# Cross-attention followed by a gated feed-forward on one core: scores, sums and first softmax product of batch 3 one loop step later

## The chip, the core and the metric

The kernel runs on one core of a Trainium2 chip. The core has five engines with a queue of instructions each: TensorE (PE in the profile; its weight loads are shown as PEld), VectorE (DVE), ScalarE (ACT), GpSimd (POOL) and SyncE (SP), which here only issues DMAs. An engine takes its instructions strictly in the order in which they were written; between engines there are semaphores only. The metric is the time of one execution on the device, in microseconds; the time before is 223.09 us, the median of three runs.

## The reference

Everything is for 8 batches and 8 heads, with 512 rows of x and 32 rows of state of width 64 in each head. Both directions of attention are computed, their results stand one under the other, and all 4352 rows of width 512 go through a gated feed-forward.

```
scores  = softmax(x @ state^T / 8)        # 512 x 32 in each head
xread   = scores @ state
sread   = softmax(state @ x^T / 8) @ x    # 32 x 64 in each head
y       = concat([xread, sread])          # 8*(512+32) rows of 512
out     = (sigmoid(y @ w_gate) * (y @ w_val)) @ w_out   # 512 -> 1536 -> 512
```

## The kernel before

The row maximum is not subtracted. The exponentials E of the scores are computed once and serve both directions: divided by their sums over the state rows they are the weights of xread, and used as the stationary operand against x they give sread. xread itself is never formed. For each batch the kernel multiplies the state with both weight matrices (SW, lines 255 to 303) and then multiplies the transposed softmax (aT) with SW, which gives gate and value directly. The sigmoid is a tanh on ScalarE (`gv_th`, L327) and one VectorE operation that adds 1 and multiplies with the value (`gv_glu`, L332); the factor 0.5 follows at the output.

The order of all instructions is written out by hand. After a long start-up for batches 0 to 2, the main loop runs b from 2 to 8 (b=8 stands for the sread rows of all batches) and, in each pass, twelve steps f of 128 hidden columns. A step has two parts on TensorE: the gate and value set of batch b (`gv_mm`, four matmuls at L317) and a third of an output tile of batch b-1 (`out_mm`, four matmuls at L348). Between them the pass prepares the next batch, nb = b+1. For nb the steps before the change do this:

- f=0 and f=6: `sw_wide`, the SW products of half the hidden columns (L259, L266), into PSUM banks that VectorE and ScalarE empty over the following steps (`sw_cp`, L303).
- f=1 and f=2: `S_mm` (eight matmuls at L147), the scores of two of the four column chunks of the batch each, into the one PSUM bank of pool `p_at` (AT), and `S_exp` (L167), their exponential on ScalarE. Score set i reads chunks 2i and 2i+1 of xT, the transposed x of nb.
- f=2 and f=3: `n_sum` (L181, L183), sums and reciprocals on VectorE. f=3: `at_Eb` (L173), four casts of E to bf16 on GpSimd.
- f=4 and f=6: `n_mul` (L200), the two softmax products on VectorE. f=5 and f=6: `aT_dma` (L221), two transposing DMAs each, from SP.
- f=6: `rd_mm` (L235 for batch 3 on), the sread product, which reads all four casts; `rd_fin` (L246, L248) writes xr, and `rd_dma` (L251) transposes it into XS. In the pass b=2 three more `rd_dma` follow at f=8.
- x is loaded two batches ahead by SP (`load_x`, L78), cast by GpSimd (`cast_x`, L116) and transposed by four DMAs from SP, one for each chunk (`at_xT_dma`, L140). For nb=3 the load of batch 5 is at f=3 and cast and transposes of batch 4 at f=6; for all other batches these are at f=0 and f=1. Batch 3's own x transposes are issued ahead of the loop.

In each step the gate and value set takes the two PSUM banks of pool `p_gv` in turn: the gate bank comes free when L327 has read it, the value bank when L332 has. SP also issues the stores of the output (L356). Its DMAs wait in one queue in the order of the program.

Of the kernel before, what the change touches and what calls it, by code (L numbers as in the profile page):

```python
# [16 lines left out]
def kernel(  # L17
# [50 lines left out]
    AT, OU, GV, SWP = (p_at, "at"), (p_out, "outp"), (p_gv, "gv"), (p_sw, "swp")  # L68
# [33 lines left out]
    def gate(landed):  # L102

        nc.gpsimd.tensor_copy(pre[:, 1:2], landed)  # L104
# [37 lines left out]
    def S_mm(b, i, place, jjs=(0, 1)):  # L142
        if b > 1:
            ps = held["S", b, i] = place[0].tile((128, 2, 2, 4, Ns), FP, name="Sp", tag=place[1])
            for c in range(2):
                for j in range(4):
                    nc.tensor.matmul(ps[:, c, :, j], xTs[b][:, j, 2 * i + c], sTz[:, b, j], start=True, stop=True)  # L147
            return
        if jjs[0] == 0:
            held["S", b, i] = place[0].tile((128, 4, 2, 2, Ns), FP, name="Sp", tag=place[1])  # L150
        ps = held["S", b, i]
        for jj in jjs:
            j = 2 * i + jj
            for c in range(4):
                e, c2 = c // 2, c % 2 * 2
                nc.tensor.matmul(ps[:, c2:c2 + 2, e, jj], xTs[b][:, j, c], sTd[:, b, 2 * j + e], start=True, stop=True)

    def half(b, i, t):

        if b > 1:  # L160
            return t[b][:, 2 * i:2 * i + 2].rearrange("p c e (j n) -> p (c e j) n", n=Ns)
        return t[b].rearrange("p c e (j n) -> p (c e) j n", n=Ns)[:, :, 2 * i:2 * i + 2]

    def S_exp(b, i):
        if b not in E1s:
            E1s[b] = ap_.tile((128, 4, 2, 128), FP, name="E1")
        nc.scalar.activation(half(b, i, E1s), held["S", b, i].rearrange("p c e j n -> p (c e j) n" if b > 1 else "p c e j n -> p (c e) j n"),  # L167
                             AF.Exp, scale=scale)
# [6 lines left out]
    def grp(b, t):  # L175

        return t if b > 1 else t.rearrange("p (g j) -> p g j", j=2)

    def n_sum(b, i):
        rs = ap_.tile((128, 16), FP, name="rs")  # L180
        nc.vector.tensor_reduce(grp(b, rs), half(b, i, E1s), AX.X, ALU.add)  # L181
        ri = held["ri", b, i] = ap_.tile((128, 16), FP, name="ri")
        nc.vector.reciprocal(ri, rs)  # L183
# [12 lines left out]
    def n_mul(b, i, eng):  # L196
        if b not in abs_:
            abs_[b] = ap_.tile((128, 4, 2, 128), BF, name="ab")
        ri, e1 = grp(b, held["ri", b, i]), half(b, i, E1s)
        (nc.gpsimd if eng is pool else nc.vector).tensor_tensor(half(b, i, abs_), e1,  # L200
                          ri.unsqueeze(len(ri.shape)).to_broadcast(e1.shape), ALU.mult)
# [7 lines left out]
    def aT_tile(b):  # L209
        if b not in aTs:  # L210
            aTs[b] = ap_.tile((128, 4, 2, 128), BF, name="aT")
        return aTs[b]
# [6 lines left out]
    def aT_dma(b, i):  # L219
        for c in range(2 * i, 2 * i + 2):  # L220
            nc.sync.dma_start_transpose(aT_tile(b)[:, c], abs_[b][:, c].rearrange("p e k -> p (e k)"))  # L221
# [4 lines left out]
    def rd_mm(b, place):  # L226

        ps = place[0].tile((128, 512), FP, name="rdp", tag=place[1])
        rd = held["rd", b] = ps[:, :2 * D + 2].rearrange("p (e d) -> p e d", e=2)
        for e in range(2):  # L230
            for c in range(4):
                for j in range(4):
                    h, o, Eb = 2 * j + e, rd[j * Ns:(j + 1) * Ns, e], Ebs[b][:, c, e, j * Ns:(j + 1) * Ns]
                    if b > 2:
                        nc.tensor.matmul(o, Eb, xs[:, c, h, :D + 1], start=(c == 0), stop=(c == 3))  # L235
                    else:
                        xh = xhs[b][:, h, c] if b in xhs else xbs[b][:, c, h]
                        nc.tensor.matmul(o[:, :D], Eb, xh, start=(c == 0), stop=(c == 3))  # L238
        for e in range(2 if b < 3 else 0):
            for c in range(4):  # L240
                nc.tensor.matmul(rd[:, e, D:], Ebs[b][:, c, e], ones, start=(c == 0), stop=(c == 3))

    def rd_fin(b):
        rd = held["rd", b]
        r2 = ap_.tile((128, 2, 1), FP, name="rr")
        nc.vector.reciprocal(r2, rd[:, :, D:])  # L246
        xr = held["xr", b] = ap_.tile((128, 2, D), BF, name="xr", bufs=4)
        nc.vector.tensor_tensor(xr, rd[:, :, :D], r2.to_broadcast((128, 2, D)), ALU.mult)  # L248

    def rd_dma(b):  # L250
        nc.sync.dma_start_transpose(XS[:, b].rearrange("p j n -> p (j n)"), held["xr", b].rearrange("p e d -> p (e d)"))  # L251
# [33 lines left out]
    def sw_wide(b, v, other=AT):  # L285

        if b not in SWs:
            SWs[b] = fp.tile((128, 2, 2, dff), BF, name="SW", bufs=2)
        lo = 768 * v
        for k, places in enumerate(((OU, other), (SWP, SWP), (SWP, SWP))):  # L290
            pss = [p[0].tile((128, 512), FP, name="swp", tag=p[1]) for p in places]
            if k < 2:
                sw_mm(pss, b, k, lo, 512, 0)
            else:
                sw_pair(pss, b, lo + 512, 256)
            for e in range(2):
                if k < 2:
                    sw_left[b, v, k, e] = (SWs[b][:, e, k, lo:lo + 512], pss[e])
                else:
                    sw_left[b, v, k, e] = (SWs[b][:, e, :, lo + 512:lo + 768], pss[e].rearrange("p (w n) -> p w n", w=2))  # L300

    def sw_cp(b, lo, w, e, cp):
        cp(*sw_left.pop((b, lo, w, e)))  # L303
# [20 lines left out]
    def gv_th(b, f):  # L324

        th = held["th", b, f] = fp.tile((128, 512), FP, name="th")[:, :n_of(b)]
        nc.scalar.activation(th, held["gv", b, f][0], AF.Tanh, scale=0.5)  # L327

    def gv_glu(b, f):
        if b not in glus:  # L330
            glus[b] = fp.tile((128, NF, n_of(b)), BF, name="glu", bufs=2, padded_shape=(128, NF, 512))
        nc.vector.scalar_tensor_tensor(glus[b][:, f], held["th", b, f], 1.0, held["gv", b, f][1], ALU.add, ALU.mult)  # L332
# [349 lines left out]
    for b in range(2, B + 1):  # L682
        nb = b + 1 if b + 1 < B else None
        for f in range(NF):

            v, q = divmod(f, 6)
            ahead = nb is not None and q == 0
            if ahead:
                if v:
                    rd_mm(nb, AT)  # L690
                sw_wide(nb, v, GV if v else AT)
                if v:
                    n_mul(nb, 1, nc.vector)
                    rd_fin(nb)
                sw_cp(nb, v, 0, v, act)
                sw_cp(nb, v, 0, 1 - v, act)
            for first in (ahead, not ahead):
                if first:
                    gv_mm(b, f, SWP if b == B and f % 2 else GV)
                    gv_th(b, f)  # L700
                    gv_glu(b, f)
                elif b < B or f < 9:
                    out_mm(b - 1, f)
            if nb is not None:
                if f in (0, 8):
                    sw_cp(nb, v, 1, 0, vec)
                if q in (1, 3, 4):
                    k = max(q + 1, 3)
                    sw_cp(nb, v, k // 2, k % 2, act)
                if f in (1, 2):  # L710
                    S_mm(nb, f - 1, AT)
                    S_exp(nb, f - 1)
                if f in (2, 3):
                    n_sum(nb, f - 2)
                elif f == 4:
                    n_mul(nb, 0, nc.vector)
                if f == 3:
                    at_Eb(nb)
                if f == (3 if nb == 3 else 0) and nb + 2 < B:
                    load_x(nb + 2, nc.sync)  # L720
                if f in (5, 6):
                    aT_dma(nb, f - 5)
                if f == 6:
                    rd_dma(nb)
                if b == 2 and f == 8:
                    for q in range(3):
                        rd_dma(q)
                if f == 0:
                    gate(held["th", b, 0][:, 0:1])
                    cast_xs(nb, 0, 4)  # L730
                    cast_xs(nb, 4, 4)
                if f == (6 if nb == 3 else 1) and nb + 1 < B:
                    cast_x(nb + 1, pool, 0, 4)
                    cast_x(nb + 1, pool, 4, 4)
                    at_xT_dma(nb + 1)
# [33 lines left out]
```

## Time and profile before

| | us |
|---|---|
| runs before, median (lowest, highest) | 223.09 (222.89, 224.12) |
| profiled execution | 223.65 |
| its span, first to last instruction | 221.9 |
| TensorE busy | 214.9 |
| ScalarE busy | 129.0 |
| VectorE busy | 118.3 |
| GpSimd busy | 53.8 |

The profile is of one execution. Times in it are counted from the start of the span; an engine's line in the order of time gives the start, the length, the engine, the line of the kernel, the operation, the tile written and the tiles read, how many such instructions are merged, and in brackets how long the engine sat idle before and what ended that. Consecutive instructions overlap a little, since their pipelines do; the advance of an engine is read from start to start. SPq is SP's queue of DMA issues; a DMA's landing is the time from its issue to the arrival of its data.

### The profile page before, as it was taken

The page shows a single profiled execution, that of the slowest core. Times are in us where ns is not written, and L with a number is a line of the kernel's source. Part 1 is how long each engine was busy: PE and PEld are TensorE (multiplying, and loading weights), DVE is VectorE, ACT ScalarE, POOL GpSimd, SP SyncE. Part 2 cuts the span into 40 slices and gives each one's busy share as a digit, 9 for nine tenths or more (in the row PEclk, how much of TensorE's full clock was granted, in tenths as well). Part 3 has the DMA queues.
Part 4 walks back from the last instruction along what each step waited for, and adds up shares of the span by engine and source line. Part 5 has one row for each costly group of instructions (what it writes and reads, how often), then busy time and mean ns, then how long its engine had stood idle before and what let it go on. Part 6 is the DMA issues. An engine that isn't in the chain of part 4 may idle for free.

```text
span 221.9 us, 4663 instructions
## 1 busy us (share of the span) xinstructions
PE 214.9 (97%) x1801; PEld 103.8 (47%) x1801; DVE 118.3 (53%) x209; ACT 129.0 (58%) x241; POOL 53.8 (24%) x90
## 2 busy tenths in 40 slices
PE   7799999999989999999999999999999999999994
PEld 2454444443444444444444454445444444466744
DVE  1889897476365546744484358353754344322301
ACT  5678877367655657656774857566756444433311
POOL 8787110470514036001800090005100000000001
PEclk9999999999999999999999999999999999999999
DMA  6999999852799555955462205420132111111113
GB/s 194 193 203 195 268 228 161 159 186 60 77 286 307 53 124 140 207 140 178 141 177 46 95 3 132 103 74 30 47 84 67 47 49 62 62 68 47 52 29 113
DMA packets 41910, 27.11 MB, mean 122 GB/s; under 512 B 24000, under 2 KB 38080, under 8 KB 41888
## 3 DMA queue, kind: packets, MB, share of 16 engines
q1 hardware_dynamic: 32544, 18.95, 36.3%
q0 software_dynamic: 9056, 7.67, 19.8%
q8 instruction: 14, 0.23, 0.4%
q10 hardware_dynamic: 288, 0.20, 0.4%
q14 instruction: 8, 0.07, 0.1%
HBM read 18.35 MB, written 8.91 MB: 123 GB/s over the span
## 4 chain that ended last, share of the span: by engine, by line
PE 89%; DMA 7%; SPq 2%; issue 0%; ACT 0%; POOL 0%; DVE 0%
PE gvp L317 37%; PE outp L348 37%; PE gvp L320 5%; PE swp L259 4%; DMA wgv<-in_moe_w_gate_dram 3%; DMA xT<-xb 2%; DMA xf<-in_x_dram 2%; SPq L140 2%; PE swp L266 2%; PE outp L370 1%; PE Sp L147 1%; PE rdp L235 1%; SPq L83 0%; PE stp L410 0%; PE rdp L238 0%
## 5 line engine op out<-in xcount | busy, mean ns | idle before, releaser
L332 DVE SCALAR_TENSOR_TENSOR glu<-th,gvp 128x512 bf16<-128x512 f32 (+1 forms) x108 | 70.5, 657 | 85.1 <-ACT th L327 68.9
L348 PE MATMUL outp<-wo,glu 128*128 128x512 bf16 x396 | 98.2, 379 | 0.0
L317 PE MATMUL gvp<-aT,SW 128*128 128x512 bf16 x384 | 96.6, 379 | 0.0
L327 ACT ACTIVATE th<-gvp 128x512 f32<-128x512 f32 (+1 forms) x108 | 61.7, 574 | 59.9 <-PE gvp L317 47.6
L317 PEld LDWEIGHTS <-SW 128*128 128x128 bf16 x384 | 36.2, 98 | 47.7 <-issue 5.6
L348 PEld LDWEIGHTS <-glu 128*128 128x128 bf16 x396 | 37.8, 98 | 42.2 <-issue 0.4
L303 ACT CAST SW<-swp 128x512 bf16<-128x512 f32 x70 | 39.2, 584 | 6.3 <-PE swp L259 4.7
L352 ACT ACTIVATE res<-outp 128x512 f32<-128x512 f32 x33 | 19.7, 597 | 15.0 <-PE outp L348 15.0
L104 POOL COPY pre<-th 128x1 f32<-128x1 f32 x5 | 0.9, 188 | 70.8 <-ACT th L327 70.8
L303 DVE CAST SW<-swp 128x512 bf16<-128x512 f32 x26 | 17.3, 684 | 1.1 <-PE swp L266 0.8
L361 POOL DMA_DIRECT2D out_dram<-res x2 | 1.1, 550 | 60.4 <-ACT res L352 60.4
L173 POOL CAST Eb<-E 128x256 bf16<-128x256 f32 x32 | 11.8, 402 | 12.0 <-ACT E L167 12.0
L116 POOL CAST xb<-xf 128x1024 bf16<-128x1024 f32 x10 | 10.6, 1087 | 11.2 <-DMA xf<-in_x_dram 7.3
L320 PE MATMUL gvp<-XS,wgv 128*128 128x256 bf16 x96 | 11.9, 273 | 0.0
L167 ACT ACTIVATE E<-Sp 128x512 f32<-128x512 f32 x16 | 9.5, 603 | 3.1 <-PE Sp L147 1.9
L320 PEld LDWEIGHTS <-wgv 128*128 128x128 bf16 x96 | 9.4, 98 | 3.0
L224 POOL CAST xs<-xf 128x1024 bf16<-128x1024 f32 x10 | 10.2, 1046 | 0.0
L181 DVE TENSOR_REDUCE rs<-E 128x16 f32<-128x512 f32 x14 | 9.4, 673 | 1.2 <-ACT E L167 1.2
L200 DVE TENSOR_TENSOR ab<-E,ri 128x512 bf16<-128x512 f32 x13 | 9.1, 709 | 0.0
L259 PE MATMUL swp<-wgv,sTc 64*32 64x512 bf16 x192 | 7.6, 381 | 0.0
L384 PE MATMUL warm<-wm 128*128 128x512 bf16 x17 | 6.0, 472 | 1.0 <-DVE wm L431 1.0
L147 PEld LDWEIGHTS <-xT 128*128 128x128 bf16 x96 | 4.4, 98 | 3.5 <-DMA xT<-xb 0.9
(71 smaller groups left out, 92.3 us busy)
## 6 DMA issues: line engine op xcount, KB each, us to landing
out_dram<-res SPq DMA_DIRECT2D x24, 256.0 KB, 3.1
xf<-in_x_dram SPq DMA_DIRECT2D x4, 1024.0 KB, 6.6
xf<-in_x_dram POOLq DMA_DIRECT2D x2, 1024.0 KB, 8.9
out_dram<-res SPq DMA_DIRECT2D x15, 128.0 KB, 1.9
wo<-in_moe_w_out_dram POOLq DMA_DIRECT2D x3, 512.0 KB, 13.7
xf<-in_x_dram SPq DMA_DIRECT2D x4, 256.0 KB, 4.0
wgv<-in_moe_w_gate_dram POOLq DMA_DIRECT2D x2, 512.0 KB, 8.5
wgv<-in_moe_w_val_dram POOLq DMA_DIRECT2D x2, 512.0 KB, 10.0
```

The source lines that it names most:

```text
L116: cp(xbs[b].rearrange("p c h d -> p h c d")[:, lo:lo + n], (xhs if b in xhs else xfs)[b][:, lo:lo + n])
L167: nc.scalar.activation(half(b, i, E1s), held["S", b, i].rearrange("p c e j n -> p (c e j) n" if b > 1 else "p c e j n -> p (c e) j n"), AF ...
L173: nc.gpsimd.tensor_copy(Ebs[b][:, c], E1s[b][:, c])
L224: pool(xs.rearrange("p c h d -> p h c d")[:, lo:lo + n, :, :D], xfs[b][:, lo:lo + n])
L259: nc.tensor.matmul(pss[e][j * Ns:(j + 1) * Ns, o:o + n], sTc[rows, b, j] if b > 1 else sTd[rows, b, 2 * j + e, e], (wg, wv)[w][rows, j, lo ...
L303: cp(*sw_left.pop((b, lo, w, e)))
L317: nc.tensor.matmul(ps, SWs[b][:, g, w, fs], aTs[b][:, :, g], start=(g == 0), stop=(g == 1))
L320: nc.tensor.matmul(ps, (wg, wv)[w][:, j, fs], XS[:, :, j], start=(j == 0), stop=(j == 3))
L327: nc.scalar.activation(th, held["gv", b, f][0], AF.Tanh, scale=0.5)
L332: nc.vector.scalar_tensor_tensor(glus[b][:, f], held["th", b, f], 1.0, held["gv", b, f][1], ALU.add, ALU.mult)
L348: nc.tensor.matmul(ops[b, c], glus[b][:, f, c * 128:(c + 1) * 128], wo[:, f], start=(f == 0), stop=(f == NF - 1))
L352: nc.scalar.activation(res, ops[b, c], AF.Copy, scale=0.5)
```

## The change

For nb=3 only, the steps of the chain scores, exponential, sums, first softmax product and casts move by one: g = f-1 takes the place of f. The score sets go to f=2 and f=3, the sums to f=3 and f=4, the casts to f=4, the first product to f=5 and the first pair of aT transposes to f=6, where the second pair already stands. The second product, the sread product and its transpose, all SW work, loads, casts of x and their transposes keep their steps. For all other batches g = f, and the order is as before. Within a step the order of the calls stays.

```diff
-                if f in (1, 2):
-                    S_mm(nb, f - 1, AT)
-                    S_exp(nb, f - 1)
-                if f in (2, 3):
-                    n_sum(nb, f - 2)
-                elif f == 4:
+                g = f - 1 if nb == 3 else f
+                if g in (1, 2):
+                    S_mm(nb, g - 1, AT)
+                    S_exp(nb, g - 1)
+                if g in (2, 3):
+                    n_sum(nb, g - 2)
+                elif g == 4:
                     n_mul(nb, 0, nc.vector)
-                if f == 3:
+                if g == 3:
                     at_Eb(nb)
                 if f == (3 if nb == 3 else 0) and nb + 2 < B:
                     load_x(nb + 2, nc.sync)
-                if f in (5, 6):
-                    aT_dma(nb, f - 5)
+                if g == 5:
+                    aT_dma(nb, 0)
                 if f == 6:
+                    aT_dma(nb, 1)
                     rd_dma(nb)
```

On each engine the number of instructions stays the same. On TensorE the two score sets of batch 3 each stand one output set and one gate and value set later; on ScalarE the second exponential moves behind the tanh and an SW cast of the next step; on VectorE each sum stands one L332 later and the two softmax products stand next to each other; on GpSimd and in SP's queue the order is unchanged.

## The prediction

> **What bounds the kernel now.** I read the page first, then the engines' waits, then the order of time around the change.
>
> ```profile
> span 221.9 us, 4663 instructions
> PE 214.9 (97%) x1801; PEld 103.8 (47%) x1801; DVE 118.3 (53%) x209; ACT 129.0 (58%) x241; POOL 53.8 (24%) x90
> PE 89%; DMA 7%; SPq 2%; issue 0%; ACT 0%; POOL 0%; DVE 0%
> ```
>
> The first line is the span, the second the busy time of each engine, the third the shares of the chain that ended last. TensorE (PE) is busy 97% of the span and carries 89% of the chain: the kernel is as long as its matmuls plus PE's holes. So the change matters only where it closes or opens a hole on PE. The waits of PE, by line, put the largest hole after the start-up here:
>
> ```profile
> PE Sp L147 <- DMA xT<-xb: 0.8, 1, 0.8
> ```
>
> One wait, once: a score matmul of L147 for a transposed x chunk. PE's order of time (start, length, instruction, idle before it):
>
> ```profile
> 58.79 0.40 PE L147 MATMUL Sp<-sTz,xT 128*128 128x64 bf16 x8
> 59.02 1.03 PE L348 MATMUL outp<-wo,glu 128*128 128x512 bf16 x4
> 59.89 1.03 PE L317 MATMUL gvp<-aT,SW 128*128 128x512 bf16 x4
> 60.75 0.28 PE L147 MATMUL Sp<-sTz,xT 128*128 128x64 bf16 x4
> 61.80 0.29 PE L147 MATMUL Sp<-sTz,xT 128*128 128x64 bf16 x4 [0.76 <-DMA xT<-xb]
> 61.92 1.03 PE L348 MATMUL outp<-wo,glu 128*128 128x512 bf16 x4
> 62.79 1.03 PE L317 MATMUL gvp<-aT,SW 128*128 128x512 bf16 x4
> 66.24 1.03 PE L317 MATMUL gvp<-aT,SW 128*128 128x512 bf16 x4
> 67.20 0.43 PE L235 MATMUL rdp<-xs,Eb 128*32 128x65 bf16 x32
> ```
>
> This is the pass b=2, from the end of step f=1 to the head of step 6, without step 4 and the output set of step 5. Eight score matmuls advance PE by 59.02-58.79 = 0.23 us. The second set takes from 60.75 to 61.92, that is 1.17 us: the hole is really 1.17-0.23 = 0.94 us (the 0.76 printed counts from a modelled end). What it waited for:
>
> ```profile
> 53.56 5.13 SPq L140 DMA_TRANSPOSE xT<-xb  x4
> 57.43 4.32 DMA xT<-xb
> ```
>
> The first is SP's queue, the second a piece of the chain that ended last. The last of batch 3's four transposes was issued at 57.43 and landed at 61.75, just ahead of the matmul at 61.80. The second score set reads chunks 2 and 3, so its last four matmuls need that one.
>
> **What the change removes: 0.94 us.** No instruction is added or taken away; batch 3's chain shifts one step. I lay PE's order out again with 0.86 us for each set of four wide matmuls (59.89 less 59.02 is 0.87; 62.79 less 61.92 as well). Step 2: output at 58.79, gate and value at 59.65, first score set at 60.52. Step 3: output 60.75, gate and value 61.61, second score set 62.48. Its last four matmuls start near 62.59, 0.84 us after the landing. Without the stall they would have started at 60.87 before, so the move can absorb at most 62.59-60.87 = 1.72 us of lateness, and closes today's 0.94. Everything PE does from step 4 on is 0.94 us earlier: the gate and value set of step 5 at 65.30 instead of 66.24, the L235 set at 66.26 instead of 67.20.
>
> **What it moves on ScalarE and GpSimd: nothing on the path.**
>
> ```profile
> 59.52 0.61 ACT L167 ACTIVATE E<-Sp 128x512 f32<-128x512 f32 x1
> 63.47 0.60 ACT L327 ACTIVATE th<-gvp 128x512 f32<-128x512 f32 x1 [0.75 <-PE gvp L317]
> 63.96 0.58 ACT L303 CAST SW<-swp 128x512 bf16<-128x512 f32 x1
> 62.78 0.74 POOL L173 CAST Eb<-E 128x256 bf16<-128x256 f32 x2 [1.84 <-ACT E L167]
> ```
>
> The tanh starts 0.68 us after its gate matmuls (62.79 to 63.47), so at 62.29; the SW cast that now precedes the second exponential starts 0.49 later and ends near 63.36, the exponential near 63.9. Both run before the tanh of step 4, whose gate matmuls now start at 63.57 (62.48+0.23+0.86) and which follows them by the same 0.68, near 64.25. GpSimd's last two Eb casts (0.74) end near 64.7; the L235 matmuls that read them come at 66.26. Cover 1.6 us, cost 0; without that cover each us of lateness would be one on PE. The two score sets share one PSUM bank: the first exponential follows the step 2 tanh, ends near 61.5, and the second score set wants the bank at 62.48. Cover 1.0.
>
> **What it moves on VectorE.** The sums go to steps 3 and 4, the first product from step 4 to step 5, right ahead of the second product of step 6.
>
> ```profile
> 67.56 0.69 DVE L332 SCALAR_TENSOR_TENSOR glu<-th,gvp 128x512 bf16<-128x512 f32 x1 [0.49 <-ACT th L327]
> 68.16 0.84 DVE L200 TENSOR_TENSOR ab<-E,ri 128x512 bf16<-128x512 f32 x1
> 69.12 0.29 DVE L248 TENSOR_TENSOR xr<-rdp,rr 128x128 bf16<-128x128 f32 x1
> 69.65 0.69 DVE L332 SCALAR_TENSOR_TENSOR glu<-th,gvp 128x512 bf16<-128x512 f32 x1 [0.24 <-ACT th L327]
> 70.95 1.03 PE L317 MATMUL gvp<-aT,SW 128*128 128x512 bf16 x4
> 87.42 0.69 DVE L332 SCALAR_TENSOR_TENSOR glu<-th,gvp 128x512 bf16<-128x512 f32 x1 [0.38 <-ACT th L327]
> 89.09 0.69 DVE L332 SCALAR_TENSOR_TENSOR glu<-th,gvp 128x512 bf16<-128x512 f32 x1
> ```
>
> A sum and its reciprocal fit between two L332 products 1.67 us apart (87.42 and 89.09, batch 4's own); steps 3 to 5 space them by 1.96 (two sets and the score set) and 1.73 (two sets), so the sums cost 0. The products: the L332 of step 5 runs at 66.62, the first softmax product at 67.22 to 67.90, the second from 67.82, and with the extra product (0.60 from start to start) xr starts at 69.12-0.94+0.60 = 68.78. The L332 of step 6, whose tanh would allow it at 68.71, then runs about 69.1 to 69.8. Its PSUM bank is wanted by the value half of step 7, half a set after 70.95-0.94 = 70.01, so near 70.44. Cover 0.6: cost 0 by these rows. But GpSimd casts at the same time:
>
> ```profile
> 67.42 2.48 POOL L116 CAST xb<-xf 128x1024 bf16<-128x1024 f32 x2 [3.90 <-PE gvp L317]
> L116 POOL CAST xb<-xf x2: 1043/1271/1499, 67.4 to 68.4; 128x1024 bf16<-128x1024 f32 x2
> 66.38 0.68 DVE L200 TENSOR_TENSOR ab<-E,ri 128x512 bf16<-128x512 f32 x1
> ```
>
> The product that ran beside those casts took 0.84 instead of 0.68, and the second cast 1.50 instead of 1.04. Both products now fall into these casts, which start when a load lands and so stay at 67.42. Lower bound 0 (each 0.16 longer still ends in time); upper bound: the second product stands behind a whole cast, 67.90+1.04 = 68.94, ends at 69.62, xr near 70.0, the L332 near 70.7, 0.3 too late. I take 0.1, nearer to the measured 0.16 than to a whole cast.
>
> The Trainium skill ("SBUF — State Buffer", section "SBUF: two separate sides") speaks against the change here: VectorE and GpSimd share one port pair, locked for a whole instruction, also by a VectorE operation with two SBUF inputs against a GpSimd operation that reads SBUF. By that rule the cost is the 0.3 of the upper bound and the gain 0.64; by the rows alone it is 0 and 0.94. The trace leans to the rule: the second cast's extra 0.46 looks like waiting out the product.
>
> **What it moves on SP.** SP's order of DMAs is the same; the first transpose pair of the softmax product now waits for VectorE's 67.90.
>
> ```profile
> 67.06 0.33 SPq L356 DMA_DIRECT2D out_dram<-res  x1
> 67.50 5.05 SPq L221 DMA_TRANSPOSE aT<-ab  x4
> 72.64 1.18 SPq L251 DMA_TRANSPOSE XS<-xr  x1
> 73.92 6.43 SPq L140 DMA_TRANSPOSE xT<-xb  x4
> 85.91 6.30 SPq L140 DMA_TRANSPOSE xT<-xb  x4
> 93.41 5.41 SPq L221 DMA_TRANSPOSE aT<-ab  x4
> L140 SPq DMA_TRANSPOSE xT<-xb x2: 1257/1264/1271, 77.8 to 79.1; - x2
> DMA to landing us min/median/max: 2.5/2.5/2.5
> 85.01 0.40 PE L147 MATMUL Sp<-sTz,xT 128*128 128x64 bf16 x8
> 102.90 1.04 PE L317 MATMUL gvp<-aT,SW 128*128 128x512 bf16 x4
> ```
>
> SP starts them at about 68.0 instead of 67.50. In these rows each group begins where the one before ends, but for a few stores, XS transposes and a load that fill the rest; I find no idle in the queue until 98.82, so all of it is 0.5 us later, while PE is 0.94 earlier. Behind it stand batch 4's x transposes: the last was issued at 79.1 and landed in 2.5, so at 81.6, now 82.1; the second score set of batch 4 (85.01) wants it half a set in, now at 84.2: cover 2.1. Batch 4's aT transposes end at 98.82 in the queue; the last of four was issued about a quarter of 5.41 ahead of that, at 97.5, and with 2.5 for the landing is there at 100.0, now 100.5, against 102.90-0.94 = 101.96: cover 1.5. Batch 3's own aT, through the queue at 72.55, now 73.05, and landed near 74.3, is first read at the head of pass b=3, some 4 us later. Cost 0.
>
> **Sum.** -0.94 + 0 + 0.1 + 0 = -0.84 us. The profiled execution lasted 223.65 us (span 221.9 and 1.75 around it), so 222.81 by its own account. It lies 0.56 above the median of the runs shown, 223.09; how long the hole is in the others no view shows, so I take the same gain there: 222.25.
>
> **The rivals.** *Another landing.* The hole depends on a landing:
>
> ```profile
> DMA to landing us min/median/max: 4.5/6.0/6.6
> ```
>
> That is the four transposes from 85.91, beside a load of 1 MB; undisturbed ones take 2.5. At 2.5 the chunk would land at 59.9, ahead of 60.87: no hole, no gain, 223.1. At 6.6 the hole would be 3.2, of which the move absorbs 1.72: 221.4. The gain passes 1.12 us (0.5%) once the landing passes 57.43 to 62.1, that is 4.7 us, counting the 0.1 on VectorE. For: the transposes follow each other beside writes of the output in every run. Against: one measured 4.32 only.
>
> *The late L332.* VectorE's two products meet both casts in the worse order, the second cast too ahead of the second product: another 1.04 us, so 1.34 of PE's time lost at step 7 against 0.94 won: 223.5. For: the 0.46 of the second cast. Against: before, the product got through between the two casts.
>
> *A late transpose (slower).* SP's half us and PE's 0.94 cut the lead of batch 4's x transposes from 3.5 (81.6 to 85.1) to 2.1. It decides once these land over 2.1 us later than forecast. If the last one lands in 6.6 instead of 2.5, as those from 85.91 did, it is 4.1 late, PE waits 2.0 us at the step 2 score set of pass b=3; with SP queueing 1.3 us longer for the four as well, close to 3.3: net 1.2 to 2.4 slower, 224.3 to 225.5, middle 224.9. For: the group was issued over 6.43 us, not 5.1, so something does slow it. Against: its last two landed in 2.5, so the engines that carry it were free again by then.
>
> *The change does not do what it says:* the order of every engine shows the shift, with no other wait; I give it nothing of its own.
>
> **How the numbers follow.** Hole closed, VectorE in time: 0.64, at 222.25 (own range 221.4 to 222.9); of it 0.36 with a landing above 4.7, since the slowed groups stand at 4.5 to 6.6, and 0.28 below. Late L332: 0.10, within 0.5%. No hole in most runs: 0.10, within. Late transpose: 0.16, of which 0.15 beyond 0.5%. So faster 0.36, within 0.5% (about what a measurement of this kernel can tell from no change) 0.49, slower 0.15. The range runs from the full 1.72 absorbed, 221.3, to the late L332, 223.6; the late transpose stays outside.
>
> **What would show it.** Right: PE's 0.8 us wait on L147 is gone and no other takes its place; the L235 set of pass b=2 near 66.3; the aT transposes of batch 3 start near 68.0; the L332 of step 6 ends before PE's step 7 value half. Wrong: an idle of PE ahead of L317 near 70.4 released by VectorE, or ahead of L147 near 84 or L317 near 102 released by a DMA; or a last x transpose of batch 3 that lands later than 62.6, so that PE still waits at step 3.

## The result

| | before | after |
|---|---|---|
| median of 21 runs, us (lowest, highest) | 223.54 (222.89, 225.18) | 222.77 (222.09, 224.37) |
| ratio after to before | | 0.9963, 95% interval 0.9945 to 0.9982 |
| profiled execution, us | 223.65 | 222.21 |
| its span, us | 221.9 | 220.4 |

The changed kernel is faster by 0.37% (0.18 to 0.55), within the 0.5% that the forecast called no change. By the ratio that is 0.83 us of 223.54; the medians lie 0.77 apart. The profiles differ by 1.5 us of span, nearly twice that, and the order of time says why.

After the change, the span, the busy time and the shares of the chain that ended last, from the page:

```profile
span 220.4 us, 4641 instructions
PE 214.4 (97%) x1779; PEld 104.3 (47%) x1801; DVE 118.1 (54%) x209; ACT 129.0 (59%) x241; POOL 53.5 (24%) x90
PE 93%; DVE 4%; issue 1%; ACT 1%
```

(The profile lacks the records of some matmuls: it has 1801 weight loads but 1779 matmuls. So the counts and the busy time of PE are a little low.)

The waits of TensorE in the same profile (total, times, longest), all that are listed:

```profile
PE warm L384 <- DVE wm L431: 1.0, 1, 1.0
PE Sp L156 <- DVE xT L135: 0.5, 2, 0.3
PE rdp L241 <- DVE ones L487: 0.2, 1, 0.2
PE xTp L132 <- POOL xf L91: 0.2, 1, 0.2
```

The wait of L147 for a transposed x chunk is gone, and no wait of the loop has taken its place: all four are of the start-up. PE's order of time after, from the head of pass b=2:

```profile
54.86 1.04 PE L317 MATMUL gvp<-aT,SW 128*128 128x512 bf16 x4
60.05 0.40 PE L147 MATMUL Sp<-sTz,xT 128*128 128x64 bf16 x8
60.28 1.03 PE L348 MATMUL outp<-wo,glu 128*128 128x512 bf16 x4
61.15 1.03 PE L317 MATMUL gvp<-aT,SW 128*128 128x512 bf16 x4
62.01 0.40 PE L147 MATMUL Sp<-sTz,xT 128*128 128x64 bf16 x8
62.24 1.03 PE L348 MATMUL outp<-wo,glu 128*128 128x512 bf16 x4
65.79 0.43 PE L235 MATMUL rdp<-xs,Eb 128*32 128x65 bf16 x32
```

Both score sets run in one piece of 0.23 us. From the first L317 set of the pass, its head, to the L235 set PE takes 65.79-54.86 = 10.93 us. In the profile of before the head is this line, and L235 started at 67.20, so it took 11.87:

```profile
55.33 1.04 PE L317 MATMUL gvp<-aT,SW 128*128 128x512 bf16 x4
```

The difference is 0.94 us. The other 0.5 us of the spans' difference lies ahead of the pass (55.33 against 54.86), in a part that the change does not touch; in all profiles of this document that start-up varies by 1.05 us, more than the gain.

One line came out otherwise than the prediction took it. The four transposes of batch 3's x, before and then after (shortest, median and longest landing):

```profile
L140 SPq DMA_TRANSPOSE xT<-xb x4: 1206/1257/1264, 53.6 to 57.4; - x4
DMA to landing us min/median/max: 2.4/2.5/4.3
```

```profile
L140 SPq DMA_TRANSPOSE xT<-xb x4: 1206/1257/1264, 53.0 to 56.9; - x4
DMA to landing us min/median/max: 2.4/2.5/2.6
```

The prediction let the last one land 4.3 us after its issue in both kernels and moved its reader. After the change it lands in 2.6, at 59.5, ahead of where the old place of the reader would have been in this run (60.87-0.47 = 60.40). So the hole may have been closed twice over, or by something other than the later reader. The windows of both kernels (us, busy times and counts of PE, PEld, DVE, ACT, POOL, the granted clock, the DMA engines' busy share, GB/s) show what went on during the landing. A DMA packet is counted in the stretch in which it starts, with its whole time and bytes, so a share can pass 1. Before:

```profile
58.50:59.50 1.00, 1.00 (x14) 0.57 (x12) 0.31 (x1) 0.94 (x2) 0.52 (x1) 1.00 1.90 139
59.50:60.50 1.00, 1.00 (x6) 0.45 (x5) 0.38 (x1) 1.00 (x3) 0.30 (x1) 1.00 0.85 18
60.50:61.50 1.00, 0.53 (x6) 0.25 (x4) 0.24 (x1) 0.72 (x2) 0.44 (x2) 1.00 0.53 186
```

After:

```profile
58.50:59.50 1.00, 1.00 (x6) 0.49 (x5) 0.69 (x1) 0.73 (x3) 0.04 (x1) 1.00 0.54 145
59.50:60.50 1.00, 1.00 (x14) 0.53 (x13) 0.00 (x0) 1.00 (x2) 0.00 (x0) 1.00 1.15 356
```

Before, packets of only 18 GB/s started in a microsecond in which two output stores and the last transpose were under way. After, it is 356, but there the transposes had landed and a load of 1 MB had been issued at 59.37, so the two are not the same work. Which other DMA stands at the start of that silence is seen from the queues (packets, MB, share of 16 engines) in the quarter of a microsecond from 59.25, before; the third line is the page's, for the whole run:

```profile
q1 hardware_dynamic: 78, 0.01, 519.4%
q8 instruction: 1, 0.02, 24.0%
q8 instruction: 14, 0.23, 0.4%
```

The second is a packet of an instruction queue, q8, which starts at 59.30. It is one of 14 in the run, which together carry 0.23 MB, some 16 KB each. TensorE has 3602 matmuls and weight loads, 14.07 times 256. The Trainium skill ("Runtime: NRT & Kernel Launch", section "Instruction fetch mechanics") has an engine's instructions fetched in blocks of 16 KiB, 256 instructions; the count and the size here agree. From the first of the 14 packets to the last TensorE begins 3180 of its matmuls and weight loads, 245 for each packet, though unevenly (164 to 338). If these packets are TensorE's, a block is due near a fixed place of its list, and the change, which puts the 16 instructions of the first score set one output set and one gate and value set later, makes that place come later in time: in the changed kernel the packet comes at 60.26, when the transposes have landed. The place is not exact: in the 14 profiles of this document the packet starts when TensorE has begun 604 to 618 of its 1801 weight loads.

### The profile page after: what moved, and what is told of

It reads as the page before. It is cut to its first block, busy times and chain, and to the rows that moved or that the text cites. A ratio compares the mean times of both kernels' runs of the same rounds, so it can differ in the third digit from the quotient of the medians.

```text
span 220.4 us, 4641 instructions
## 1 busy us (share of the span) xinstructions
PE 214.4 (97%) x1779; PEld 104.3 (47%) x1801; DVE 118.1 (54%) x209; ACT 129.0 (59%) x241; POOL 53.5 (24%) x90
## 4 chain that ended last, share of the span: by engine, by line
PE 93%; DVE 4%; issue 1%; ACT 1%
PE outp L348 38%; PE gvp L317 38%; PE gvp L320 5%; PE swp L259 4%; PE warm L384 2%; PE swp L266 1%; PE Sp L147 1%; PE outp L370 1%; PE rdp L235 1%; DVE rs L181 1%; DVE ab L193 1%; DVE rs L187 1%; PE aTp L207 1%; PE Sp L156 0%; DVE ab L200 0%
## 5 line engine op out<-in xcount | busy, mean ns | idle before, releaser
L332 DVE SCALAR_TENSOR_TENSOR glu<-th,gvp 128x512 bf16<-128x512 f32 (+1 forms) x108 | 70.4, 656 | 84.4 <-ACT th L327 69.4
L348 PE MATMUL outp<-wo,glu 128*128 128x512 bf16 x374 | 95.7, 379 | 1.2
L317 PE MATMUL gvp<-aT,SW 128*128 128x512 bf16 x384 | 96.7, 380 | 0.0
L317 PEld LDWEIGHTS <-SW 128*128 128x128 bf16 x384 | 36.1, 98 | 47.9 <-issue 5.6
L147 PEld LDWEIGHTS <-xT 128*128 128x128 bf16 x96 | 4.3, 98 | 2.6
```

What stands on the lines that cost most here:

```text
L317: nc.tensor.matmul(ps, SWs[b][:, g, w, fs], aTs[b][:, :, g], start=(g == 0), stop=(g == 1))
L348: nc.tensor.matmul(ops[b, c], glus[b][:, f, c * 128:(c + 1) * 128], wo[:, f], start=(f == 0), stop=(f == NF - 1))
```

## The experiments

Two theories stood after the first pair of profiles. *Absorbed*: the later reader takes up the late landing, as predicted. *Moved fetch*: the landing itself is no longer late, since TensorE's instruction fetch, the packet above, no longer meets the transpose. Besides them stood the prediction's terms for VectorE and SP.

### Is the hole there in every run?

The kernel before, unchanged, in two more profiles.

> The kernel before, unchanged, profiled once more. Theory (the hole belongs to the order of the program): PE again waits for the last x transpose of batch 3 at the second score set of pass b=2, 0.7 to 1.2 us from start to start beyond the 0.23 of a score set, with a landing of 4 us or more. Rival (the hole is a chance event of the DMA engines): the last transpose lands in 2.5 to 2.7 us, and there is no wait of PE on L147 or one below 0.2 us.

> The same as before_look, once more: theory, a wait of PE on L147 of 0.5 us or more with a landing of 4 us or more; rival, a landing of 2.5 to 2.7 and no wait.

Measured: a wait of L147 of 0.68 and 0.71 us, landings of 4.25 and 4.30. PE's order of time in the first, where the two halves of the second score set start 0.95 apart instead of 0.12:

```profile
60.33 0.28 PE L147 MATMUL Sp<-sTz,xT 128*128 128x64 bf16 x4
61.28 0.29 PE L147 MATMUL Sp<-sTz,xT 128*128 128x64 bf16 x4 [0.68 <-DMA xT<-xb]
```

The instruction packet came at 58.79 in it, ahead of the hole, with the output set of step 2 at 58.60. The hole is there in all three profiles of this kernel: it belongs to the order of the program, not to chance.

### The second score set alone

```diff
-                if f in (1, 2):
-                    S_mm(nb, f - 1, AT)
-                    S_exp(nb, f - 1)
-                if f in (2, 3):
-                    n_sum(nb, f - 2)
-                elif f == 4:
+                w = 1 if nb == 3 else 0
+                if f in (1, 2 + w):
+                    i = 0 if f == 1 else 1
+                    S_mm(nb, i, AT)
+                    S_exp(nb, i)
+                if f in (2, 3 + w):
+                    n_sum(nb, 0 if f == 2 else 1)
+                if f == 4:
                     n_mul(nb, 0, nc.vector)
-                if f == 3:
+                if f == 3 + w:
                     at_Eb(nb)
```

> Of the change, only the second score set of batch 3 with its exponential, its sum and the GpSimd casts moves one step later; first score set, first sum, first product and its transposes stay where they were. Theory (the whole gain is the hole ahead of the second score set): ratio to before 0.996 to 0.997, as the full change, and no wait of PE on L147 unless the landing passes 4.9 us. Rival (something else that the change moves brings part of it): 0.998 to 1.000, or a hole that stays.

Measured: ratio 0.9976 (0.9955 to 0.9997), just outside the 0.996 to 0.997 expected and with an interval that covers nearly the whole of the rival's range too, so the time alone decides nothing. The landing stays late, and PE does not wait for it:

```profile
L140 SPq DMA_TRANSPOSE xT<-xb x4: 1205/1257/1264, 53.1 to 57.0; - x4
DMA to landing us min/median/max: 2.4/2.5/4.3
```

Its PE in order of time:

```profile
62.12 0.40 PE L147 MATMUL Sp<-sTz,xT 128*128 128x64 bf16 x8
66.69 0.42 PE L266 MATMUL swp<-wgv,sTc 64*32 64x512 bf16 x8
67.24 1.02 PE L317 MATMUL gvp<-aT,SW 128*128 128x512 bf16 x4
```

So the later reader alone closes the hole, by absorbing: 10.96 us from the pass's head to L235. The L266 set then takes 0.55 us to the next L317 instead of 0.36 (67.48 to 67.84 in before_look): this kernel has the second sum and the first product in one step, and the L332 of step 5 is late by 0.2.

### The first product back in its step

```diff
-                elif g == 4:
+                if f == 4:
                     n_mul(nb, 0, nc.vector)
...
-                if g == 5:
+                if f == 5:
                     aT_dma(nb, 0)
```

> The change, but with the first softmax product back in step 4 and its transposes in step 5, as before. The scores stay late, so the hole is closed as in the change. VectorE then has sum, reciprocal and product between the L332 of steps 4 and 5, some 2.2 us of work from start to start in 1.73: theory: the L332 of step 5 is 0.4 late and PE waits 0.3 to 0.4 us ahead of the gate and value set of step 6, so the ratio to before is 0.9975 to 0.9985, half of the gain. Rival (the place of the product is free, VectorE has room everywhere): no new wait, 0.996 to 0.997.

Measured: ratio 0.9961 (0.9943 to 0.9978), no wait on L147, and the same 0.54 from L266 (66.72) to L317 (67.26). The cost is there at 0.19 us, half of what was expected, but the ratio is in the range of the rival. It could not show there: 0.19 us is 0.09%, about half of the interval's arm.

### TensorE's list shortened, the scores left where they were

Eight of the seventeen warm-up matmuls of the start-up are left out, which compute nothing that is used.

```diff
-    warm(1, SWP)
...
-    warm(1, GV)
...
-    warm(2, AT)
...
-    warm(1, SWP)
-    warm(1, SWP)
...
-    warm(2, OU)
```

> The kernel before with the scores in their old steps, but with eight of the seventeen warm-up matmuls of the start-up left out (they compute nothing that is used). TensorE's list is 16 instructions shorter ahead of the loop, as many as the first score set has. Theory (the hole comes from a 16 KB instruction fetch of TensorE's own, which is due at a fixed place in its list and here meets the last x transpose of batch 3): the fetch at 59.3 comes 1.5 to 1.7 us later, near 60.8 in the frame of before, the last transpose lands in 2.5 to 2.7, and PE's wait on L147 in pass b=2 is gone although no score set was moved; ratio to before 0.995 to 0.998, if the start-up is not slower without the warm-up. Rival (the two stores behind the transposes, or the place of the score set itself, slow the transpose): landing 4.2 to 4.4 and a wait of 0.7 as before, ratio 0.999 to 1.001.

Measured: the instruction packet at 60.27, that is 4.82 us behind the pass's head at 55.45, where it was 3.97 before. It came 0.85 later, not the 1.5 to 1.7 expected, but that was enough: the last transpose landed in 2.5 us, with no wait on L147 and both score sets in their old steps. PE in order of time,

```profile
58.91 0.40 PE L147 MATMUL Sp<-sTz,xT 128*128 128x64 bf16 x8
59.15 1.03 PE L348 MATMUL outp<-wo,glu 128*128 128x512 bf16 x4
60.87 0.40 PE L147 MATMUL Sp<-sTz,xT 128*128 128x64 bf16 x8
66.38 0.43 PE L235 MATMUL rdp<-xs,Eb 128*32 128x65 bf16 x32
```

and its four transposes:

```profile
L140 SPq DMA_TRANSPOSE xT<-xb x4: 1206/1257/1264, 54.0 to 57.8; - x4
DMA to landing us min/median/max: 2.4/2.5/2.5
```

From the head to L235 it is 10.93, as in the changed kernel. The two stores behind the transposes, the rival, are still there. The ratio, 0.9993 (0.9973 to 1.0012), misses the 0.995 to 0.998 expected and is not better than before. In its profile the granted clock fell to 0.87 in the first 13 us, and PE waited longer in the start-up, 1.0 us instead of 0.5 for L156 and 0.5 for an SW cast; the head stands 0.1 to 0.6 later than in the four profiles with the list and score steps of before (54.83 to 55.33). That the start-up loses what the pass wins is read from this one profile.

### The same list lengthened in the changed kernel

The six `warm` lines above with twice their matmuls, in the kernel after.

> The kernel after the change with these eight warm-up matmuls doubled, so TensorE's list is 16 instructions longer ahead of the loop. Theory: the fetch comes back to where it was before the change, just after the start of the output set of step 2, on top of the last x transpose: landing 4 us or more again, but no wait of PE on L147, since the second score set stands one step later and can take a landing of up to 5.1 us. Rival (the fetch has no part): landing 2.5 to 2.7 as after the change.

Measured: a landing of 4.4 again, no wait on L147, 10.93 from head to L235. Its four transposes:

```profile
L140 SPq DMA_TRANSPOSE xT<-xb x4: 1206/1257/2457, 54.1 to 57.9; - x4
DMA to landing us min/median/max: 2.4/3.1/4.4
```

The packet came at 58.56, 2.69 us behind the head, so further ahead than the old place that was expected, and it met two transposes: the third, issued at 56.6, took the 4.4, and the last 3.6. Moving TensorE's list by 16 instructions takes the late landing away (fewer_warm) and brings it back, while the other engines' lists stay, so the fetch has a part in it; and the changed kernel bears it. The one run took 223.25 us, so no gain in time is shown for this variant.

### SP's queue pushed later

The prediction costed SP's delay at nothing by a cover ahead of batch 4's scores. Three XS transposes go ahead of batch 4's x transposes, in both kernels.

```diff
-                if b == 2 and f == 8:
-                    for q in range(3):
-                        rd_dma(q)
...
+                    if nb == 3:
+                        for q in range(3):
+                            rd_dma(q)
                     at_xT_dma(nb + 1)
```

> The kernel after the change, with the three late XS transposes of pass b=2 (batches 0 to 2) taken from step 8 to step 6, ahead of batch 4's x transposes in SP's queue, which so start 3.7 us later. Theory (the cover of batch 4's x transposes is what the profiles show: the last one landed near 80.7 and is wanted at 83.7, 3.0 us): PE waits 0.5 to 1.0 us on L147 at the second score set of pass b=3, ratio to before 0.999 to 1.001. Rival (the cover is larger, the transposes are not the next thing to bind): no wait, ratio 0.996.

> The same move of the three XS transposes in the kernel before. Theory: its cover is 3.5 us, so PE waits 0.1 to 0.5 us on L147 in pass b=3, less than in the changed kernel, besides the 0.7 in pass b=2. Rival: no second wait, or one as long as in the changed kernel.

Measured: the kernel before has no second wait, where 0.1 to 0.5 us was expected. The changed one has two on L147, one for each score set, and one of L317 that was not expected; its ratio, 1.0041 (1.0020 to 1.0061), is above the 0.999 to 1.001 expected:

```profile
PE Sp L147 <- DMA xT<-xb: 0.9, 2, 0.4
PE gvp L317 <- DVE glu L332: 0.4, 1, 0.4
```

The first of the two on L147, and SP's queue ahead of it:

```profile
82.41 0.28 PE L147 MATMUL Sp<-sTz,xT 128*128 128x64 bf16 x4
83.12 0.29 PE L147 MATMUL Sp<-sTz,xT 128*128 128x64 bf16 x4 [0.44 <-DMA xT<-xb]
79.30 5.14 SPq L140 DMA_TRANSPOSE xT<-xb  x4
```

Each score set takes 0.6 us longer from start to start. The same 3.7 us in the queue cost before nothing and after 1.2: the change did use up cover that the next batch had. Not all of it is the moved order: this group starts 24.21 us behind the pass's head (79.30-55.09), 0.91 more than in the kernel before (78.13-54.83), where the first pair of kernels differ by 0.47, and the softmax products that it stands behind were late in this run. The third wait is the prediction's late L332. VectorE and GpSimd in that run, around steps 5 to 7:

```profile
66.66 2.48 POOL L116 CAST xb<-xf 128x1024 bf16<-128x1024 f32 x2 [2.23 <-PE rdp L235]
66.99 2.70 DVE L200 TENSOR_TENSOR ab<-E,ri 128x512 bf16<-128x512 f32 x2
70.01 0.68 DVE L332 SCALAR_TENSOR_TENSOR glu<-th,gvp 128x512 bf16<-128x512 f32 x1
70.74 0.59 PE L317 MATMUL gvp<-aT,SW 128*128 128x512 bf16 x2 [0.37 <-DVE glu L332]
```

The two products took 2.70 us instead of 1.29, beside two casts that began 0.33 us ahead of them.

### Products and casts

The changed kernel in two more profiles, and two variants in which products and casts cannot hold up that L332.

> The kernel after the change, once more, beside the two variants below. Theory: the hole ahead of the second score set is gone (no wait of PE on L147), the last x transpose of batch 3 lands in 2.5 to 2.7 as its fetch has moved; ratio to before 0.996 to 0.997. Whether PE waits for the L332 of step 6 hangs on when GpSimd's casts of batch 4 start against the two softmax products: a cast that starts less than 0.6 us ahead of the first product or during it makes that L332 late (PE waits up to 0.5), one that starts during the second does not. Rival (that wait belongs to the moved XS transposes of xT4_late_after alone): never here.

> One more look at the kernel after the change: no wait of PE on L147; the L332 of step 6 late or not by the rule named for after_look.

```diff
                 if v:
-                    n_mul(nb, 1, nc.vector)
+                    if nb != 3:
+                        n_mul(nb, 1, nc.vector)
                     rd_fin(nb)
...
                 if f == 6:
+                    if nb == 3:
+                        n_mul(nb, 1, nc.vector)
                     aT_dma(nb, 1)
```

> The change, with batch 3's second softmax product behind the L332 of step 6 instead of ahead of it; its transposes are not due in SP's queue before about 70. Theory: the L332 of step 6 has one product less ahead of it and is never late whatever GpSimd does, so no wait of PE on VectorE there; ratio to before 0.995 to 0.9965, at or below after_look by up to 0.2%. Rival (the products cost nothing in most runs): the same ratio as after_look.

```diff
                 if f == (6 if nb == 3 else 1) and nb + 1 < B:
+                    if nb == 3:
+                        gate(held["th", b, 6][:, 0:1])
                     cast_x(nb + 1, pool, 0, 4)
```

> The change, with GpSimd's two casts of batch 4 held until the tanh of step 6 (one more tiny copy on GpSimd), so that they start after the two products. Theory (products and casts lock each other out): both products last 0.68 to 0.70, both casts 1.03 to 1.06, no wait of PE on VectorE; ratio as second_late. Rival (the long products have another cause): a product of over 0.8 again.

Measured, with the changed kernel's first profile in the first row; the last column is PE's time from L235 to the L266 set of the next pass's head, which is 12.05 to 12.06 in all three profiles of before:

| run | ratio to before | casts begin | products, us | L235 to L266, us |
|---|---|---|---|---|
| after | 0.9963 (0.9945 to 0.9982) | 67.70 | 0.69, 0.69 | 12.06 |
| after_look | 0.9969 (0.9955 to 0.9982) | 67.30 | 1.11, 1.52 | 12.44 |
| after_look2 | one run | 68.29 | 0.69, 1.55 | 12.06 |
| second_late | 0.9959 (0.9947 to 0.9971) | 66.65 | 1.21, 0.69 | 12.06 |
| gated_cast | 0.9971 (0.9948 to 0.9994) | 68.98 | 0.68, 0.68 | 12.06 |

No run has a wait on L147. VectorE and GpSimd in after_look, and then in gated_cast:

```profile
67.30 2.48 POOL L116 CAST xb<-xf 128x1024 bf16<-128x1024 f32 x2 [2.08 <-PE rdp L235]
67.78 2.55 DVE L200 TENSOR_TENSOR ab<-E,ri 128x512 bf16<-128x512 f32 x2
71.38 0.59 PE L317 MATMUL gvp<-aT,SW 128*128 128x512 bf16 x2 [0.23 <-DVE glu L332]
```

```profile
66.84 1.29 DVE L200 TENSOR_TENSOR ab<-E,ri 128x512 bf16<-128x512 f32 x2
68.98 2.03 POOL L116 CAST xb<-xf 128x1024 bf16<-128x1024 f32 x2 [0.37 <-DMA xf<-in_x_dram]
```

The casts of gated_cast by themselves (shortest, median and longest, ns):

```profile
L116 POOL CAST xb<-xf x2: 1042/1042/1043, 69.0 to 70.0; 128x1024 bf16<-128x1024 f32 x2
```

Kept apart, products and casts take 0.68 and 1.04; together up to 1.5 each. The first product of after_look, at 67.78, lasted until the first cast (67.30 to 68.34) was over and 0.55 more, and the second until 0.55 after the second cast. In pass b=2 of the 14 profiles eleven products began while a cast ran, and each ended 0.54 or 0.55 us after that cast. That is the rule of the Trainium skill ("SBUF — State Buffer", section "SBUF: two separate sides"), that such a pair locks each other out for a whole instruction, and here the trace agrees with it. What decides is when batch 4's load lands against the products. The bracket of after_look's cast names L235, but the load behind it landed at 67.19, 0.11 us ahead of the cast, and the casts start 0.11 us behind that landing in every ungated profile; in the table's ungated rows they start between 66.65 and 68.29. The expectation of after_look had one point too strict: in after_look2 the casts began during the first product, but the L332 of step 6 was done at 70.87, just ahead of the value half at 70.93, so PE did not wait. Both variants have no wait of PE there. second_late has the lowest ratio measured, but its interval overlaps that of the changed kernel, so it is not shown to be faster than that; its median (222.29) lies 0.94 us under before, the one of gated_cast (222.25) 0.98.

## Why the prediction was right

- **The bound.** TensorE, so that only its holes count. Confirmed: in all 14 profiles PE's time splits into a start-up that ends between 54.83 and 55.88, the stretch to L235, the stretch to the L266 set of the next pass's head (12.05 unless a late L332 lengthens it) and a rest of 142.55 to 142.65; only xT4_late_after has more, 143.79. The change moves the second and, in some runs, the third.
- **The hole, -0.94 us.** 11.87 to 10.93, as forecast, in the first pair of profiles; 11.78 to 11.83 in the three other profiles with the old score steps and the old list, so 0.85 to 0.94. In those four profiles the last transpose landed in 4.25 to 4.35, so the landings above 4.7, on which the forecast had put 0.36 for a gain above 0.5%, did not come.
- **How it closes.** The prediction had the later reader absorb a landing that stays at 4.3 us. That holds where the landing stays late (second_only, more_warm_after). In the changed kernel itself it wasn't needed: the fetch had moved, and the landing was 2.6. Either suffices alone (second_only, fewer_warm). So the time is as forecast although this step of the account did not happen; that is partly luck. The rival "another landing" took the landing as chance; it hangs on TensorE's list, and the change moves that list.
- **ScalarE and GpSimd, 0.** The last Eb casts ended at 64.2 and L235 came at 65.8: cover 1.6, as forecast.
- **VectorE, +0.1.** In the first profile of after it is 0, with the L332 of step 6 done at 69.05 and its bank wanted near 69.97. In the five profiles with the change's order of VectorE and ungated casts (after, after_look, after_look2, more_warm_after, xT4_late_after) it is 0, 0.38, 0, 0 and 0.53, 0.18 on average. The term was of the right size, but a mean over two cases rather than a cost of each run, and 0.16 is no price: the product of 0.84 us too ended 0.55 after the cast in which it began (68.46). The late L332 was real, and cost 0.4 to 0.5, not the 1.34 of the rival.
- **SP, 0.** The first aT transpose stood 0.30 us behind L235 before and 67.51-65.79 = 1.72 after: 1.42 lost against PE, where 0.5+0.94 were forecast. It hid, as forecast; xT4_late_after shows what it took. The rival "a late transpose" had for it that batch 4's group was issued over 6.43 us in the kernel before. An instruction packet at 75.18 met it there: its first two transposes landed in 4.4 and 3.8, and PE did not wait.
- **Sum.** -0.84 forecast, -0.83 measured by the ratio, with an interval from 0.40 to 1.23. An agreement to 0.01 is luck. The time was forecast at 222.25 from a median of 223.09 over three runs; that of 21 is 223.54, and the changed kernel's 222.77.

Left open: why a fetch holds up transposes in flight. That the packets are TensorE's is inferred from their moving with its list; no view names their engine. How much a meeting costs goes with how long the transpose has been in flight. After the change the packet at 74.20 meets batch 4's first transpose 0.3 us after its issue, and that lands in 2.8; the XS transpose ahead of it, issued at 72.65 and 1.55 us in flight, lands in 3.7.

## What to carry to other kernels

A wait of a fully busy engine is worth its length from start to start, and a move closes no more of it than the work that it puts in between. Before moving work on a long instruction list, look at which instruction fetches lie beside DMA transposes: here sixteen instructions more or fewer, even in the start-up, decided whether they met. And where two engines hold each other up, the cost of bringing their work together is a question of when a load lands, so read several profiles before giving it one number.

## What the hardware showed that was not expected

A 16 KB packet of the instruction queue that moves with TensorE's list, beside a DMA transpose in flight: batch 3's x transposes land in 4.2 to 4.4 us instead of 2.5. All six profiles in which the packet comes between 58.5 and 59.3 have such a landing (four with the order of before, second_only and more_warm_after), and none of the eight in which it comes after 60. The transpose had been in flight for 1.8 to 1.9 us in the six, and for 2.46 or more in the eight. In five of the six, packets of only 18 or 19 GB/s start in the microsecond that begins a quarter of a microsecond after it; in more_warm_after it is 119, so that silence is not part of every meeting.

The same holds for the other transposes. In the 14 profiles, 71 have a packet of that queue start 1.0 to 2.1 us after their issue, and all 71 land in 3.3 to 4.6 us. Where it starts 2.3 to 2.6 us after the issue, they land in 2.3 to 2.6, but for three beside a 1 MB load.
